# The copy of an attention block's weighed sums out of PSUM: from VectorE to ScalarE

## The chip, the cores and the metric

The kernel runs on one core of a Trainium2 chip. What is measured is the device time of one execution in microseconds (us), as the median of several runs. Five engines work side by side, each through its own instructions in order: TensorE (PE in the profile; its weight loads are listed apart as PEld), VectorE (DVE), ScalarE (ACT), GpSimd (POOL), and SyncE (SP), which here issues most DMAs. They wait for each other by semaphores.

## The reference

A transformer block on 2048 rows of width 576: LayerNorm, attention with 32 heads of 18 columns, and a gated feed-forward part.

```python
def _A_ref(x, wqkv, wo):
    B, S, D = x.shape                      # 1, 2048, 576
    H = 32; Dh = D // H                    # 18
    qkv = (x @ wqkv).reshape(B, S, 3, H, Dh).transpose(2, 0, 3, 1, 4)
    q, k, v = qkv[0], qkv[1], qkv[2]
    scores = jnp.einsum("bhqd,bhkd->bhqk", q, k) * Dh ** -0.5
    p = _softmax(scores, axis=-1)
    o = jnp.einsum("bhqk,bhkd->bhqd", p, v)
    return o.transpose(0, 2, 1, 3).reshape(B, S, D) @ wo

x = A_x
h = x + _A_ref(_layernorm(x), A_wqkv, A_wo)
h2 = h + _B_ref(_layernorm(h), B_w_gate, B_w_up, B_w_down)   # gelu(x@gate) * (x@up) @ down
```

## The kernel before

**Blocks and steps.** The attention is cut into 32 blocks: 8 groups of four heads, and in each group 4 chunks of 512 queries. The loop over `n` goes through the blocks, the loop over `kt` through 16 key steps of 128 keys. In a step TensorE makes four score tiles, one a head, keys down and queries across (L665, `score`), ScalarE turns each into its exponentials in the buffers `pes` (L667), and TensorE multiplies these with the values and adds the result to one PSUM bank, `acc`, which is `bank3` in the instructions (L673, `weigh`). The weighing of a step runs during the next step, in two halves of 256 queries. `acc` takes all 16 steps of a block; every head has 32 of its 128 rows, and the row behind a head's 18 sums holds the sum of its weights.

**Maxima.** Softmax needs a query's largest score. It comes from a second set of score tiles, queries down and keys across, which run one and a half blocks ahead (`maxima`, `max_bank`): TensorE makes the tile (L615), and VectorE reduces it to one maximum a row (L625). One tile in eight goes another way: ScalarE writes its Relu to SBUF (L619), and VectorE combines that with the partner tile in one instruction (L623). A block needs 64 such tiles, that is 48 reductions, 8 Relus and 8 combined instructions.

**PSUM.** The score tiles of both kinds share seven banks, taken in turn (`m_ring`: `bank0` to `bank2` and `quad0` to `quad3`). TensorE can write a tile into a bank only when ScalarE or VectorE is done with the tile of seven turns before.

**Order.** In this stage the order on PE, ACT, DVE and POOL is the order in which the program is written. Two strings set it, one for even and one for odd `kt`:

```python
STEPS = ("ssmsmmfwmsw", "mssmssmfwwm")
OUT_AT = STEPS[0].rindex("w")
```

Here `s` is a score tile with its exponential, `m` a tile for maxima with its reduction, `w` one half of the weighing, and `f` filling work. The last `w` of step 0 ends the weighing of the block before, and right behind it comes the first part of `out_block`, with the copy out of `acc` (L688). The next block's first weighing, which overwrites `acc`, is the first `w` of step 1; between them stand, in step 1, four scores and three tiles for maxima.

**What reads the copy.** `out_block` goes on in three parts. The copy's result `oT` is read by a DMA that picks out the sums of weights (L691); GpSimd inverts them (L698 and the lines behind it), two DMAs spread the result over the rows, and GpSimd multiplies and splits (L711 to L713), before SyncE sends the rows to `XT`. For the last two blocks the copy is already on ScalarE.

Of the kernel before, what the change touches and what calls it, by code (L numbers as in the profile page):

```python
# [31 lines left out]
def tile_block(  # L32
# [18 lines left out]
    nc = tc.nc  # L51
# [5 lines left out]
    TB = min(512, S)  # L57
# [624 lines left out]
    def out_block(n, acc):  # L682

        g, qc = divmod(n, NB)
        oT = oTs[n % 2]
        (nc.scalar.copy if n >= NS - 2 else nc.vector.tensor_copy)(oT, acc[:, :TB])  # L688
        R = 4 * TB // P
        rc = small.tile([P, R], F32, tag="rc", name="rc")  # L690
        (nc.scalar if n == NS - 1 else nc.sync).dma_start(rc, oT.rearrange("(h c) q -> h c q", c=32)[:, DH].rearrange(  # L691
            "h (p q) -> h p q", q=R))
        yield
        if n < NS - NB:
            den, rc = rc, small.tile([P, R], F32, tag="rp", name="rp")
            re = small.tile([P, R], F32, tag="re", name="re")
            for c in range(0, R, 4):
                nc.gpsimd.tensor_tensor(rc[:, c : c + 4], den[:, c : c + 4],  # L698
                                        minus_one.to_broadcast([P, 4]), op=ALU.pow)
            nc.gpsimd.tensor_mul(re, den, rc)  # L700
            nc.gpsimd.tensor_scalar(re, re, -1.0, 2.0, op0=ALU.mult, op1=ALU.add)
            nc.gpsimd.tensor_mul(rc, rc, re)
        else:
            nc.vector.reciprocal(rc, rc)
        rd = rc_dram[n % 2]
        nc.sync.dma_start(rd, rc)
        nc.sync.dma_start(rcb, rd.rearrange("(h p) q -> h (p q)", h=4).unsqueeze(1)
                         .to_broadcast([4, 32, TB]))
        yield
        if n < NS - 2:  # L710
            nc.gpsimd.tensor_mul(oT, oT, rcb)  # L711
            nc.gpsimd.tensor_copy(ohl[:, 0], oT)
            nc.gpsimd.tensor_sub(ohl[:, 1], oT, ohl[:, 0])  # L713
        else:
            nc.vector.tensor_mul(oT, oT, rcb)
            (nc.scalar.copy if n == NS - 1 else nc.vector.tensor_copy)(ohl[:, 0], oT)
            nc.vector.tensor_sub(ohl[:, 1], oT, ohl[:, 0])
        sl = slice(qc * TB, (qc + 1) * TB)
        for hh in range(4):
            f, end = (4 * g + hh) * DH, (4 * g + hh + 1) * DH  # L720
            r = 32 * hh
            while f < end:
                c, p = divmod(f, P)
                k = min(end - f, P - p)
                if c < NK:
                    nc.sync.dma_start(XT[p : p + k, c : c + NK + 2 : NK + 1, sl], ohl[r : r + k])
                else:
                    other = nc.gpsimd if n >= NS - 2 else nc.sync
                    nc.sync.dma_start(XT[p : p + k, NK, sl], ohl[r : r + k, 0])
                    other.dma_start(XT[TAIL + p : TAIL + p + k, NK, sl], ohl[r : r + k, 1])  # L730
                f += k
                r += k

    NS = NG * NB
# [525 lines left out]
    for n in range(NS):  # L1260
        g, qc = divmod(n, NB)
        acc = singles[3]
        late = n > NS - NB
        for kt in range(NT):
            heads = iter(range(4))
            halves = weigh(*prev) if prev is not None else iter(())
            for step_no, step in enumerate(STEPS[kt % 2]):
                if step == "s":
                    score(n, kt, next(heads))
                elif step == "m":  # L1270
                    take(mxs)
                elif step == "w":
                    take(halves)
                    if kt == 0 and step_no == OUT_AT and prev is not None:
                        ob = out_block(prev[0], prev[2])
                        next(ob)
                else:
                    if n < NS - 1 or kt < 11:
                        take(fill, 2)
                    take(side)  # L1280
# [29 lines left out]
    run(side)  # L1310
    run(weigh(*prev))
    ob = out_block(prev[0], prev[2])
    next(ob)
    for _ in fill:
# [103 lines left out]
```

## Time and profile before

| | |
|---|---|
| three runs | 2606.03, 2608.47, 2609.94 us; median 2608.47 us |
| profiled execution, first to last instruction | 2604.1 us |
| median of the runs less that span | 4.4 us |
| PE busy in the span | 2579.3 us (99%) |
| DVE busy | 2010.0 us (77%) |
| ACT busy | 1661.3 us (64%) |
| POOL busy | 818.9 us (31%) |
| copies at L688 on VectorE / on ScalarE | 30 / 2 |
| one such copy, from its start to its end | 681 ns on VectorE, 585 ns on ScalarE |

The profile's rows stand in a section below. Times there are in us from the span's start. Busy time counts an instruction from its start to its end; two instructions that follow each other on one engine can overlap, as the second may start before the first has ended, so the spacing of the ends of a row of instructions without a pause is the time that each one holds the engine. A row that ends in `x2` is two instructions, from the start of the first to the end of the second.

### The profile page before, as it was taken

Reading aid. Unit: us, or ns where it says so; the run is one execution under the profiler, and the core shown is the slowest. Engines: PE = TensorE matmul, PEld = TensorE weight load, DVE = VectorE, ACT = ScalarE, POOL = GpSimd, SP = SyncE. Lnnn points to the kernel's source line nnn. Section 1 sums busy time; section 2 is a strip of 40 time slices with the busy share of each in tenths; the row PEclk is TensorE's granted clock in tenths of the full one; section 3 lists DMA queues with packets and bytes.
Section 4 is the critical chain, followed back from the end, with each engine's and each line's share of the span. In section 5 each row is a group of like instructions: output and inputs, shape, how many; then the busy total and the mean of one; then the engine's idle time right before and its main releaser. Section 6 shows DMA issues by size and latency. Waiting matters only on the chain.

```text
span 2604.1 us, 53642 instructions
## 1 busy us (share of the span) xinstructions
PE 2579.3 (99%) x20765; PEld 1198.2 (46%) x20765; DVE 2010.0 (77%) x3886; ACT 1661.3 (64%) x3124; POOL 818.9 (31%) x1146
## 2 busy tenths in 40 slices
PE   8999999999999999999999999999999999999999
PEld 4543333333333333333335555555555555555555
DVE  8479999999999999999867675757565656565653
ACT  6229999999999999999774543424243433333332
POOL 4302532322223232324585432323232323222221
PEclk9999999999999999999999999999999999999999
DMA  8621010101001010101135410101010101010110
GB/s 227 154 77 45 17 47 17 44 19 39 20 23 41 16 43 16 47 16 32 38 64 116 83 34 30 34 30 34 30 34 30 34 30 34 30 34 30 34 56 37
DMA packets 170193, 118.23 MB, mean 45 GB/s; under 512 B 88664, under 2 KB 147564, under 8 KB 169938
## 3 DMA queue, kind: packets, MB, share of 16 engines
q1 hardware_dynamic: 161198, 98.47, 14.2%
q0 software_dynamic: 8608, 16.33, 2.6%
q8 instruction: 162, 2.65, 0.4%
q14 instruction: 93, 0.76, 0.1%
q10 hardware_dynamic: 132, 0.01, 0.0%
HBM read 80.05 MB, written 15.01 MB: 37 GB/s over the span
## 4 chain that ended last, share of the span: by engine, by line
PE 92%; DVE 4%; POOL 1%; DMA 1%; issue 1%; ACT 1%; SPq 0%; POOLq 0%; ACTq 0%
PE bank L673 19%; PE bank L1125 15%; PE more L1125 15%; PE bank L300 11%; PE more L300 8%; PE quad L615 7%; PE bank L615 6%; PE quad L300 4%; PE quad L665 4%; DVE mx L625 3%; PE bank L665 3%; DVE nat L688 1%; DMA A<-qk_hi 0%; POOL A L1055 0%; ACT A L155 0%
## 5 line engine op out<-in xcount | busy, mean ns | idle before, releaser
L667 ACT ACTIVATE WK<-quad 128x512 f32<-128x512 f32 x1170 | 656.2, 621 | 23.4 <-PE quad L665 21.0
L673 PE MATMUL bank<-WK,V 128*32 128x256 f32 x8192 | 606.6, 388 | 2.7 <-DVE nat L688 0.6
L625 DVE TENSOR_REDUCE mx<-quad 128x1 f32<-128x512 f32 x836 | 553.8, 684 | 9.0 <-PE quad L665 1.5
L667 ACT ACTIVATE WK<-bank 128x512 f32<-128x512 f32 x878 | 504.9, 622 | 11.1 <-PE bank L665 9.3
L625 DVE TENSOR_REDUCE mx<-bank 128x1 f32<-128x512 f32 x716 | 477.1, 684 | 33.5 <-PE bank L615 26.4
L300 PEld LDWEIGHTS <-WK 128*128 128x128 f16 x3456 | 338.2, 98 | 88.3
L1125 PEld LDWEIGHTS <-W 128*128 128x128 f16 x2394 | 234.3, 98 | 278.3
L673 PEld LDWEIGHTS bank<-WK,V 128*32 128x32 f32 x8192 | 190.0, 108 | 268.2 <-issue 201.3
L300 PE MATMUL more<-W,WK 128*128 128x288 f16 x1728 | 235.2, 286 | 0.0
L300 PE MATMUL bank<-W,WK 128*128 128x288 f16 x1728 | 235.2, 286 | 0.0
L698 POOL TENSOR_TENSOR rp<-rc,minus_one 128x4 f32<-128x4 f32 x112 | 111.2, 1012 | 383.9 <-DMA rc<-nat 383.9
L1125 PE MATMUL bank<-X,W 128*128 128x512 f16 x792 | 223.8, 379 | 0.0
L1125 PE MATMUL bank<-V,W 128*128 128x512 f16 x720 | 202.4, 379 | 0.0
L993 POOL TENSOR_TENSOR A<-A 128x384 f32<-128x384 f32 x136 | 138.1, 1036 | 200.2 <-DMA A<-in_B_w_up_dram 83.7
L615 PE MATMUL quad<-W 54*128 54x512 f16 x514 | 191.0, 382 | 0.2 <-DVE mx L625 0.2
L615 PEld LDWEIGHTS <-W 54*128 54x128 f16 x1024 | 74.5, 94 | 241.3 <-issue 226.8
L1139 POOL TENSOR_TENSOR WK<-tmp,WK 128x512 f16<-128x512 f32 x73 | 88.5, 1212 | 305.8 <-ACT WK L1136 305.6
L615 PEld LDWEIGHTS <-A 54*128 54x128 f16 x1024 | 71.1, 94 | 231.0 <-issue 216.7
L1143 ACT COPY tmp<-more 128x512 f32<-128x512 f32 x36 | 20.9, 582 | 238.3 <-PE more L1125 203.4
L665 PE MATMUL quad<-A 56*128 56x512 f16 x584 | 172.1, 380 | 0.3
L615 PE MATMUL quad<-A 54*128 54x512 f16 x462 | 171.6, 382 | 0.1
L665 PE MATMUL quad<-W 56*128 56x512 f16 x586 | 167.5, 380 | 0.1
(348 smaller groups left out, 4122.3 us busy)
## 6 DMA issues: line engine op xcount, KB each, us to landing
A<-in_B_w_down_dram SPq DMA_DIRECT2D x8, 1152.0 KB
nat<-rc SPq DMA_DIRECT2D x32, 256.0 KB
A<-in_B_w_gate_dram SPq DMA_DIRECT2D x64, 128.0 KB
A<-in_B_w_up_dram SPq DMA_DIRECT2D x64, 128.0 KB
qk_hi<-tmp SPq DMA_DIRECT2D x36, 128.0 KB
qk_lo<-tmp SPq DMA_DIRECT2D x36, 128.0 KB
out_dram<-nat SPq DMA_DIRECT2D x16, 288.0 KB
X<-nat SPq DMA_DIRECT2D x100, 36.0 KB
```

The source lines that it names most:

```text
L300: nc.tensor.matmul(dst, a, b, start=(i == 0), stop=(i == len(pairs) - 1))
L615: nc.tensor.matmul(pm[:, :TB], Q[r, q0 : q0 + P], keys, start=True, stop=True)
L625: nc.vector.tensor_reduce(dst, pm[:, :TB], axis=AX.X, op=ALU.max)
L665: nc.tensor.matmul(pS[:, :TB], K[r, kt * P : (kt + 1) * P], Q[r, qc * TB : (qc + 1) * TB], start=True, stop=True)
L667: nc.scalar.activation(pes[(2 * kt + hh // 2) % NPE][:, hh % 2], pS[:, :TB], AF.Exp, scale=ex_reg)
L673: nc.tensor.matmul(acc[32 * hh : 32 * hh + 32, qs], Vg[n // NB][:, kt * G4 + hh * VC : kt * G4 + hh * VC + 32], pes[(2 * kt + hh // 2) % N ...
L688: (nc.scalar.copy if n >= NS - 2 else nc.vector.tensor_copy)(oT, acc[:, :TB])
L698: nc.gpsimd.tensor_tensor(rc[:, c : c + 4], den[:, c : c + 4], minus_one.to_broadcast([P, 4]), op=ALU.pow)
L993: op(W8[:, d], W8[:, a], W8[:, b])
L1125: nc.tensor.matmul(bank, w, x_, start=start and i == 0, stop=i == len(mm) - 1, skip_group_check=not start)
L1139: nc.gpsimd.tensor_sub(hl[:, 2 * i + j], v, hh[:, 2 * i + j])
L1143: nc.scalar.copy(xg, g[0])
```

## The change

The condition at L688 is gone. Blocks 30 and 31 had their copy on ScalarE before and keep it there; for blocks 0 to 29 it moves from VectorE to ScalarE.

```diff
         g, qc = divmod(n, NB)
         oT = oTs[n % 2]
-        (nc.scalar.copy if n >= NS - 2 else nc.vector.tensor_copy)(oT, acc[:, :TB])
+        nc.scalar.copy(oT, acc[:, :TB])
         R = 4 * TB // P
```

On ScalarE, at the start of block 10, these rows stood in a row before: the fourth exponential of step 0 is the one that reads `quad3`, those behind it belong to steps 1 and 2 (`WK` holds `pes`, and `nat` the rows of the Relu).

```order
L667 ACTIVATE WK_81<-bank2_68 128x512
L619 ACTIVATE nat_77<-quad0_73 128x512
L667 ACTIVATE WK_81<-quad3_76 128x512
L667 ACTIVATE WK_81<-bank1_67 128x512
L667 ACTIVATE WK_81<-bank2_68 128x512
L667 ACTIVATE WK_81<-quad1_74 128x512
L667 ACTIVATE WK_81<-quad2_75 128x512
```

The same place now, where `nat` is also the buffer `oT`:

```order
L667 ACTIVATE WK_81<-bank2_68 128x512
L619 ACTIVATE nat_77<-quad0_73 128x512
L667 ACTIVATE WK_81<-quad3_76 128x512
L688 COPY nat_77<-bank3_69 128x512
L667 ACTIVATE WK_81<-bank1_67 128x512
L667 ACTIVATE WK_81<-bank2_68 128x512
L667 ACTIVATE WK_81<-quad1_74 128x512
L667 ACTIVATE WK_81<-quad2_75 128x512
```

The copy stands between the last exponential of step 0 and the four of step 1. On VectorE it leaves the place between two reductions, here at the start of the same block:

```order
 L625 TENSOR_REDUCE mx_6079<-quad1_74 128x1
 L625 TENSOR_REDUCE mx_6079<-quad2_75 128x1
-L688 COPY nat_77<-bank3_69 128x512
 L625 TENSOR_REDUCE mx_6079<-bank0_66 128x1
 L623 ISA nat_77,mx_6079<-quad0_73,nat_77 128x512
```

VectorE's other rows keep their order. TensorE's order is the same throughout; only the first weighing of a block, and the readers of `oT`, wait for ScalarE where they waited for VectorE.

## Rows read from the trace of the kernel before

**Rows 1.** The page: busy time by engine, and the chain that ended last by engine.
```profile
PE 2579.3 (99%) x20765; PEld 1198.2 (46%) x20765; DVE 2010.0 (77%) x3886; ACT 1661.3 (64%) x3124; POOL 818.9 (31%) x1146
PE 92%; DVE 4%; POOL 1%; DMA 1%; issue 1%; ACT 1%; SPq 0%; POOLq 0%; ACTq 0%
```

**Rows 2.** One attention block: PE, PEld, DVE, ACT, POOL busy; granted clock; DMA share; GB/s.
```profile
530.24:566.08 35.84, 35.76 (x388) 11.54 (x384) 35.32 (x67) 35.73 (x73) 8.37 (x14) 1.00 0.08 21
```

**Rows 3.** Line L688, who waited for it: us in total, times.
```profile
  PEld bank L673: 15.8, 31
```

**Rows 4.** ScalarE in order of time at a block's start: start, duration, what.
```profile
565.16 0.67 ACT L619 ACTIVATE nat<-quad 128x512 f32<-128x512 f32 x1
565.64 0.68 ACT L667 ACTIVATE WK<-quad 128x512 f32<-128x512 f32 x1
566.23 1.08 ACT L667 ACTIVATE WK<-bank 128x512 f32<-128x512 f32 x2
567.20 1.10 ACT L667 ACTIVATE WK<-quad 128x512 f32<-128x512 f32 x2
...
570.92 1.57 ACT L667 ACTIVATE WK<-quad 128x512 f32<-128x512 f32 x3
```

**Rows 5.** TensorE in order of time around the same block's start.
```profile
561.28 0.39 PE L665 MATMUL quad<-A 56*128 56x512 f16 x1
...
563.93 0.39 PE L615 MATMUL quad<-A 54*128 54x512 f16 x1
564.24 0.64 PE L673 MATMUL bank<-WK,V 128*32 128x256 f32 x8
...
565.71 0.60 PE L665 MATMUL bank<-A 56*128 56x512 f16 x2
...
566.38 0.38 PE L615 MATMUL quad<-A 54*128 54x512 f16 x1
...
566.82 1.07 PE L673 MATMUL bank<-WK,V 128*32 128x256 f32 x16
...
568.35 0.37 PE L615 MATMUL quad<-nat,A 54*128 54x512 f16 x1
568.63 0.37 PE L615 MATMUL quad<-A 54*128 54x512 f16 x1
568.93 0.64 PE L673 MATMUL bank<-WK,V 128*32 128x256 f32 x8
...
570.40 0.60 PE L665 MATMUL quad<-A 56*128 56x512 f16 x2
```

**Rows 6.** VectorE in order of time around the same block's start.
```profile
562.92 1.46 DVE L625 TENSOR_REDUCE mx<-quad 128x1 f32<-128x512 f32 x2
...
566.08 0.68 DVE L688 COPY nat<-bank 128x512 f32<-128x512 f32 x1
566.68 0.68 DVE L625 TENSOR_REDUCE mx<-bank 128x1 f32<-128x512 f32 x1
...
567.88 0.69 DVE L625 TENSOR_REDUCE mx<-quad 128x1 f32<-128x512 f32 x1
```

**Rows 7.** ScalarE in order of time around the copy of block 30.
```profile
1348.62 0.58 ACT L688 COPY nat<-bank 128x512 f32<-128x512 f32 x1
1349.10 1.09 ACT L667 ACTIVATE WK<-bank 128x512 f32<-128x512 f32 x2
```

**Rows 8.** ScalarE in order of time: a copy of the same size behind another instruction.
```profile
1397.31 1.26 ACT L1013 ACTIVATE W<-A,p_s_m 128x1152 f16<-128x1152 f32 x1
1398.46 0.58 ACT L1146 COPY tmp<-bank 128x512 f32<-128x512 f32 x1
```

**Rows 9.** TensorE at the starts of blocks 3 and 30, with idle time and its releaser.
```profile
315.34 0.39 PE L615 MATMUL quad<-W 54*128 54x512 f16 x1
315.93 0.84 PE L673 MATMUL bank<-WK,V 128*32 128x256 f32 x10 [0.21 <-DVE nat L688]
...
1301.96 0.64 PE L673 MATMUL bank<-WK,V 128*32 128x256 f32 x8 [0.21 <-DVE nat L688]
```

## The prediction, made before the changed kernel was run

> **What bounds the kernel now.** I read the page first, then the busy times of single attention blocks, then the three engines in order of time around a block's start. The page says that TensorE is busy 99% and carries 92% of the chain that ended last; VectorE has 4% of it and ScalarE 1% [rows 1]. That invites the thought that ScalarE has time to spare. It is an average over stages. In one attention block of 35.84 us TensorE, VectorE and ScalarE are busy 35.76, 35.32 and 35.73 us [rows 2]: all three look full, so busy time does not say which of them sets the pace. The granted clock is 1.00 there, and nothing in the change bears on it.
>
> Spacings tell more. ScalarE's four rows from 565.16 on end at 565.83, 566.32, 567.31 (two) and 568.30 (two) [rows 4]. The spacing of the ends is 0.49 us, and only between 566.32 and 567.31 is there a little more (0.99 for two, of which 0.01 to 0.02 is a pause). A double step has eight exponentials and one Relu, so ScalarE needs 9 x 0.49 = 4.41 us for it. TensorE's regular double step, from the first score of one odd step to that of the next, takes 565.71 - 561.28 = 4.43 us [rows 5]. **ScalarE is therefore full to about 0.02 us in a double step**, and tied to TensorE in a loop: the last tile for maxima of an even step is held until the fourth exponential of the odd step before has freed its bank (568.30 to 568.35, a hand-over of 0.05) [rows 4, 5], then come the weighing, the scores of the next odd step, and their exponentials. VectorE is behind in that race: it has pauses, for instance two reductions that take 1.46 us together [rows 6], where two without a pause would take 0.60 from start to start and 0.68 for the last, 1.28.
>
> At a block's start this pattern is broken. The double step from 565.71 to 570.40 takes 4.69 us, 0.26 more [rows 5]. Both parts of that are VectorE's: the first weighing waits for the copy, which ends at 566.76, and starts at 566.82, and because the copy delays the reductions by 0.60, the tile at 568.63 waits for the reduction that ends at 568.57, so that the second weighing starts at 568.93 [rows 5, 6]. In total 31 weight loads waited 15.8 us for L688 [rows 3]. That wait is what the change can win back.
>
> **The change part by part.** *Removed from VectorE:* 30 copies of 0.68 us, each holding it for 0.60 us (566.08 to 566.68) [rows 6]. VectorE's reductions at a block's start come 0.60 us earlier, and the tile at 568.63 no longer waits for one. Elsewhere VectorE waits for TensorE once or twice in a double step, so the time is not worth anything there.
>
> *Added to ScalarE:* 30 copies, each behind the fourth exponential of step 0. **How long one holds ScalarE** is shown by rows from other stages: behind an instruction that ends at 1398.57 the copy ends at 1399.04, 0.47 later [rows 8]; and the two exponentials behind a copy that ends at 1349.20 end at 1350.19, 0.495 each [rows 7]. I take 0.475, and 0.495 for the first exponential behind it. The sums are there in time: VectorE began to read them at 566.08 [rows 6], and ScalarE reaches the copy at about 566.12, 0.48 after the start at 565.64 [rows 4]. Queued behind the copy are the four exponentials of step 1, and behind those, through their banks, TensorE.
>
> *A regular block's start, laid out anew.* The fourth exponential of step 0 ends at 566.32 [rows 4]. The copy ends at 566.32 + 0.475 = 566.80, so the first weighing, 0.06 behind it as before, starts at 566.86 where it was 566.82. The four exponentials of step 1 end 0.495 + 3 x 0.49 = 1.965 later, at 568.76, where before it was 568.30: 0.46 late. The tile that waits for the fourth starts at 568.81. From the last tile to the weighing it is 564.24 - 563.93 = 0.31 us where nothing else is waited for [rows 5], which gives 569.12 in place of 568.93. **So a regular block gets longer by 0.19 us**: VectorE's two waits (0.26) are gone, and ScalarE's (0.45) stand in their place. Nothing later takes it back: the next double step's first score comes at 570.59, its exponential can start 0.52 later, as before (570.40 to 570.92) [rows 4, 5], and end 0.60 behind that, at 571.71; ScalarE's own queue would have it end at 568.76 + 6 x 0.49 = 571.70. Both engines are then 0.19 late, and the old rhythm goes on from there. Of the 30 moved copies 27 stand at such a start: 27 x 0.19 = +5.1 us.
>
> *Three irregular starts.* In blocks 3, 29 and 30 TensorE is already late for other reasons and ScalarE waits for it; there the copy fits into ScalarE's pause. The last tile stands at 315.34 and the weighing at 315.93 [rows 9], 0.59 apart, where 0.31 is the least: 0.28 is won. The second of VectorE's two waits may go too; at a regular start the first is 566.82 - 566.38 - 0.31 = 0.13 [rows 5], and the second the rest of 0.26, so 0.13 more. Of the three starts the first and the last stand in [rows 9]; all show the same idle 0.21 in front of the weighing. That is 0.28 to 0.41 each, -0.8 to -1.2; I take -1.0.
>
> *With one answer:* the readers of `oT` (the DMA at L691, GpSimd's L711) get it 0.04 us later and are not waited for within the block; the two copies that were on ScalarE before don't change; no DMA is moved.
>
> **Sum:** +5.1 - 1.0 = +4.1 us. On the profiled span that is 2604.1 + 4.1 = 2608.2; the median of the runs lies 4.4 above the span, so 2612.6 us, 0.16% more than 2608.47. A measurement of this kernel can tell about 0.2% (5.2 us) from no change.
>
> *Bounds.* The one price that no row shows in place is a copy within a full row of exponentials. From below: if starts and not ends were what counts, the copy and each exponential would take 0.48; step 1's first exponential would start at 566.60 in place of 566.23, the delay would be 0.37, the weighing at 569.03, and the sum 27 x 0.10 - 1.0 = +1.7. From above: if the copy held ScalarE for its whole 0.58 us [rows 7], a block would lose 0.30, and the sum would be 27 x 0.30 - 0.8 = +7.3. The row nearest to the place is that of [rows 8], a copy behind a busy ScalarE; it gives the value taken. The ends drift away from the starts, by some 0.01 an instruction, until the next pause: 0.67 and 0.68 long at 565.16 and 565.64 [rows 4], against 0.60 behind a pause. So the engine is slower than its starts say, and I stay with the ends. The Trainium skill (Perfetto Trace Analysis, Per-instruction lifecycle) has the profiled end behind the write's acknowledgement, and lets the next instruction begin to fetch before that, once the one before has executed; by that reading the starts would be the better clock, and the sum +1.7.
>
> **The rivals.** *A, slower: the copy holds ScalarE for its whole run.* Place: the four exponentials behind it. Price: +7.3 us, 2615.8. It decides when the hold passes 0.515 us, since 27 x (hold - 0.285) - 1.0 reaches 5.2 there. For it: no row shows a copy in a full row of exponentials, and the forecast lies only 1.1 us below the point. Against it: the row in which the next exponential starts 0.48 behind the copy's start [rows 7].
>
> *B, faster: VectorE sets the pace.* Then 0.60 us comes free in each of 30 blocks: -18 us, 2590. For it: it is the only other engine with a share in the chain [rows 1], and 35.32 of 35.84 us busy [rows 2]. Against it: the pauses in [rows 6]. The Trainium skill (Perfetto Trace Analysis, Optimizing Scalar/DVE Operations) advises moving work to ScalarE where VectorE is saturated; by that this change would be rival B, but [rows 4] show ScalarE at least as full.
>
> *C, faster: the waits of the block's start vanish and ScalarE catches up.* 27 x 0.26 + 1.0 = 8.0 us less, 2600.5. It needs ScalarE to make up 0.46 us within one double step, where the rows leave it 0.02; it holds only if exponentials can come closer together than 0.49, which I have not seen in a full stretch.
>
> **How the numbers follow.** The forecast's case has 0.55, A (with all that lies above 0.2%) 0.33, C 0.08, B 0.04. The time is that of the forecast, 2612.6. Its own range is that of the bounds' nearer part, 2610 to 2613.7 (0.2%). The range of 8 in 10 reaches up to A and a little beyond, 2617, and down to where the runs scatter below the lower bound (+1.7 is 2610), 2606.5; B and C, 0.12, are left out. Faster by over 0.2%: B and C, 0.12. Slower by over 0.2%: A, 0.33. Within: 0.55.
>
> **What the profile of the changed kernel would show.** At a regular start no weight load waits for VectorE's L688, and ScalarE's row reads exponential, copy, exponentials with ends 0.47 to 0.48 and 0.49 apart. The double step with the copy takes 4.88 us in place of 4.69, all others 4.43, and a block 36.03 in place of 35.84. VectorE shows pauses at the block's start. I am wrong if the double step takes 4.43 to 4.6 (C), if blocks get shorter by more than 0.3 (B), or if the copy's end lies over 0.515 behind the end before it (A).

## The result, and the profile after

The changed kernel takes 2613.36 us (median of 15 runs, 2611.23 to 2617.86), the kernel before 2608.47 (median of 15, 2606.03 to 2612.63). The ratio is 1.002, with an interval from 1.0013 to 1.0028, so the change costs between 3.4 and 7.3 us. Forecast were +4.1 us and 2612.6. The kernel is slower beyond the scatter; whether by more or less than 0.2% the interval does not say.

The page of the changed kernel, span, busy time and chain by engine:

```profile
span 2615.4 us, 53644 instructions
PE 2585.5 (99%) x20765; PEld 1200.8 (46%) x20765; DVE 2002.3 (77%) x3856; ACT 1670.4 (64%) x3154; POOL 818.5 (31%) x1146
PE 93%; ACT 2%; DMA 1%; DVE 1%; POOL 1%; issue 1%; SPq 1%; ACTq 0%; POOLq 0%; DVEq 0%
```

Beside [rows 1] VectorE has lost its share of the chain (4% to 1%) and ScalarE has gained one. The span has grown by 11.3 us, more than the median (4.9). The first score tiles of the blocks, in both traces, say where:

| stretch | before | after | difference |
|---|---|---|---|
| to the first score of block 0 | 202.90 | 205.09 | +2.2 |
| block 0 | 37.13 | 40.06 | +2.9 |
| blocks 1 to 28 | 1004.50 | 1010.09 | +5.6 |
| block 29 to the last step of block 31 | 132.45 | 133.67 | +1.2 |
| the rest, to the last instruction | 1227.12 | 1226.46 | -0.7 |

The first copy that was moved runs in block 1, so what lies ahead of it is not the change. Among the experiments below that alter only this copy (e3 to e6, and e12), block 0 begins from 201.8 to 203.2 and takes 37.1 to 38.7 us; the last section says what lengthened it here. **The change itself is in the third line.** That line holds 27 times 0.21 us, less 0.46 won in block 3, and some 0.4 of scatter: blocks 14, 21 and 28 of the changed kernel took 0.1 to 0.3 longer than their neighbours, and block 15 before it 0.3.

A stretch of one block, as in [rows 2], in the same columns (PE, PEld, DVE, ACT, POOL busy; clock; DMA share; GB/s), and who waits for the copy (us, times):

```profile
533.55:569.60 36.05, 35.82 (x388) 11.72 (x385) 35.04 (x66) 36.02 (x75) 8.38 (x14) 1.00 0.09 22
```
```profile
L688 ACT COPY nat<-bank x32: 586/677/678, 248.0 to 1392.6; 128x512 f32<-128x512 f32 x32
...
  PEld bank L673: 15.3, 29
```

A block takes 36.05 us in place of 35.84. TensorE's loads still wait for the copy as long as in [rows 3] (15.3 us in 29 waits, 15.8 in 31 before): the wait has changed its engine, not its size. It is not a price either, as e3 shows below.

ScalarE at the start of block 10, to be held against [rows 4]:

```profile
571.99 0.68 ACT L667 ACTIVATE WK<-quad 128x512 f32<-128x512 f32 x1
572.46 0.68 ACT L688 COPY nat<-bank 128x512 f32<-128x512 f32 x1
572.93 1.20 ACT L667 ACTIVATE WK<-bank 128x512 f32<-128x512 f32 x2
573.90 1.21 ACT L667 ACTIVATE WK<-quad 128x512 f32<-128x512 f32 x2
574.85 1.24 ACT L667 ACTIVATE WK<-bank 128x512 f32<-128x512 f32 x2
```

TensorE there, against [rows 5]:

```profile
572.05 0.60 PE L665 MATMUL bank<-A 56*128 56x512 f16 x2
...
572.72 0.38 PE L615 MATMUL quad<-A 54*128 54x512 f16 x1
573.19 1.07 PE L673 MATMUL bank<-WK,V 128*32 128x256 f32 x16
...
575.17 0.39 PE L615 MATMUL quad<-A 54*128 54x512 f16 x1
575.48 0.64 PE L673 MATMUL bank<-WK,V 128*32 128x256 f32 x8
...
576.95 0.60 PE L665 MATMUL quad<-A 56*128 56x512 f16 x2
```

And VectorE, against [rows 6], with the idle time in front of an instruction and its releaser in brackets:

```profile
573.69 0.68 DVE L625 TENSOR_REDUCE mx<-quad 128x1 f32<-128x512 f32 x1
574.62 0.69 DVE L625 TENSOR_REDUCE mx<-bank 128x1 f32<-128x512 f32 x1 [0.25 <-PE bank L665]
```

The last exponential of step 0 ends at 572.67, the copy at 573.14, the four exponentials behind it at 574.13 (two) and 575.11 (two). The weighing starts 0.05 behind the copy, at 573.19. The last tile for maxima starts 0.06 behind the fourth exponential, at 575.17, and the second weighing 0.31 later. VectorE, no longer late, waits for TensorE. The double step takes 576.95 - 572.05 = 4.90 us; it was 4.69.

### The profile page after: what moved, and what is told of

Same layout as the page of the kernel before. It is cut to its first block, busy times and chain, and to the rows that moved or that the text cites. A ratio compares the mean times of both kernels' runs of the same rounds, so it can differ in the third digit from the quotient of the medians.

```text
span 2615.4 us, 53644 instructions
## 1 busy us (share of the span) xinstructions
PE 2585.5 (99%) x20765; PEld 1200.8 (46%) x20765; DVE 2002.3 (77%) x3856; ACT 1670.4 (64%) x3154; POOL 818.5 (31%) x1146
## 4 chain that ended last, share of the span: by engine, by line
PE 93%; ACT 2%; DMA 1%; DVE 1%; POOL 1%; issue 1%; SPq 1%; ACTq 0%; POOLq 0%; DVEq 0%
PE bank L673 19%; PE bank L1125 15%; PE more L1125 15%; PE bank L300 11%; PE more L300 8%; PE quad L615 8%; PE bank L615 6%; PE quad L300 5%; PE quad L665 4%; PE bank L665 3%; ACT WK L667 2%; DVE mx L625 0%; DMA A<-qk_hi 0%; SPq L729 0%; DMA nat<-qk_hi 0%
## 5 line engine op out<-in xcount | busy, mean ns | idle before, releaser
L667 ACT ACTIVATE WK<-quad 128x512 f32<-128x512 f32 x1170 | 665.7, 636 | 23.1 <-PE quad L665 21.7
L667 ACT ACTIVATE WK<-bank 128x512 f32<-128x512 f32 x878 | 513.5, 636 | 12.3 <-PE bank L665 11.6
```

Of the source, the lines that this page charges most:

```text
L667: nc.scalar.activation(pes[(2 * kt + hh // 2) % NPE][:, hh % 2], pS[:, :TB], AF.Exp, scale=ex_reg)
```

## The experiments

The theory is that a block's length is set by a path that goes from ScalarE's exponentials over the freed PSUM banks to TensorE's tiles and weighings and back, and that the copy on ScalarE lies on it with its whole hold. The rivals: the loss is a hand-over at the block's start, not ScalarE's time (H); it is the sum of ScalarE's work in a block, wherever it stands (S); VectorE sets the pace (V).

"Block" below is the time from the first score of block 10 to that of block 11, "start" the double step of steps 1 and 2. Before and after stand for comparison; medians are in us, with the median of the kernel before from the same chip, and e8 to e11 are single runs, of which the blocks are read and not the times.

| kernel | block 10 from, to | block | start | median, before beside it |
|---|---|---|---|---|
| before | 563.26, 599.10 | 35.84 | 4.69 | |
| after | 569.60, 605.65 | 36.05 | 4.90 | 2613.36, 2608.47 |
| e1 | 569.42, 605.87 | 36.45 | 4.69 | 2626.14, 2608.89 |
| e2 | 571.22, 607.63 | 36.41 | 4.69 | 2623.22, 2608.89 |
| e3 | 561.36, 596.99 | 35.63 | 4.48 | 2602.55, 2608.89 |
| e4 | 564.98, 601.09 | 36.11 | 4.96 | 2616.32, 2609.08 |
| e5 | 567.11, 603.25 | 36.14 | 4.99 | 2616.32, 2609.08 |
| e6 | 564.40, 600.24 | 35.84 | 4.69 | 2608.15, 2609.08 |
| e7 | 568.77, 604.81 | 36.04 | 4.90 | 2613.99, 2608.89 |
| e8 | 563.58, 599.30 | 35.72 | 4.57 | 2605.87, 2609.39 |
| e9 | 569.25, 605.58 | 36.33 | 4.68 | 2622.33, 2609.39 |
| e10 | 570.06, 606.33 | 36.27 | 4.69 | 2621.13, 2609.39 |
| e11 | 565.71, 601.79 | 36.08 | 4.68 | 2613.22, 2609.39 |
| e12 | 561.16, 596.74 | 35.58 | 4.43 | 2601.26, 2608.67 |

### What each copy costs: eight columns on ScalarE (e3) and on VectorE (e12)

e3, against the kernel after; in e12 the same edit is made to VectorE's copy of the kernel before:

```diff
-nc.scalar.copy(oT, acc[:, :TB])
+C = TB if n >= NS - 2 else 8
+nc.scalar.copy(oT[:, :C], acc[:, :C])
```

> The changed kernel, with 8 of 512 columns copied in blocks 0 to 29 (the rest of the sums is not copied, so the rows behind it are computed from old values); the copy's place, its waits and who waits for it stay. Theory, full row: the copy's cost goes with the time it holds ScalarE; the double step at the block's start falls from 4.90 to 4.43 to 4.50 us, a block to 35.60 to 35.67, 5 to 7 us less than before the change. Rival, hand-over: the waits stay, so the double step stays near 4.9 and the time near that of the changed kernel, +5 us.

> The kernel before, with 8 of 512 columns copied by VectorE in blocks 0 to 28 and 29 (the rest of the sums is not copied, so the rows behind it are computed from old values). It prices VectorE's copy as the run with 8 columns on ScalarE priced ScalarE's. If VectorE's copy costs the 0.26 us that I had put down to its two waits, a block takes 35.58 to 35.65 us, and the whole 6 to 8 us less than before. If ScalarE and TensorE alone set the length of a block and VectorE's copy only stood beside them, 35.84.

e3 gave a ratio of 0.9978 (0.9968 to 0.9987), e12 0.9976 (0.9966 to 0.9986). ScalarE in e3, at the start of block 10, and VectorE in e12:

```profile
563.74 0.68 ACT L667 ACTIVATE WK<-quad 128x512 f32<-128x512 f32 x1
564.22 0.26 ACT L689 COPY nat<-bank 128x8 f32<-128x8 f32 x1
564.33 1.14 ACT L667 ACTIVATE WK<-bank 128x512 f32<-128x512 f32 x2
```
```profile
563.98 0.16 DVE L689 COPY nat<-bank 128x8 f32<-128x8 f32 x1
564.06 0.68 DVE L625 TENSOR_REDUCE mx<-bank 128x1 f32<-128x512 f32 x1
```

In e3 the place, the waits and the waiting instructions are those of the changed kernel; only the hold is short (564.42 to 564.48), and the block falls from 36.05 to 35.63. H is out: it is the time on ScalarE that costs. e12's start takes 4.43 us, the regular double step, so 35.58 is a block without any price for the copy. Against it **VectorE's copy costs 0.26 us a block and ScalarE's 0.47**, which is its hold. In e3 TensorE's loads still wait 10.2 us for the copy, in 27 waits, while a block costs only 0.05 us more than in e12: the sum of these waits does not measure what the copy costs.

### One instruction more on ScalarE in mid-block (e1, e9)

In e1, made from the kernel before, the Relu of step 12 runs twice, with the same input and output; in e9 the added line is the same with `row2` for its output and `tmp3[:, 0]` for its input.

```diff
 nc.scalar.activation(row, pm[:, :TB], AF.Relu)
+if (t, kc) == (1, 1):
+    nc.scalar.activation(row, pm[:, :TB], AF.Relu)
```

> The kernel before, with the copy left on VectorE, and one Relu a block, the one of step 12 in the middle of the block, run twice over the same buffer. Theory, full row: ScalarE has no time to spare anywhere in a block, so one more instruction of 0.49 us costs about 0.45 us a block wherever it stands: block 36.3 us in place of 35.84, +13 us in all. Rival, hand-over: what the changed kernel lost comes from ScalarE and TensorE waiting for each other at a block's start; an instruction in mid-block then costs 0 to 0.05 us a block, under 2 us. Rival, VectorE paces: 0.

> The kernel before, with one more Relu of 512 columns a block on ScalarE in step 12, from a buffer in SBUF that nothing writes in this stage, into a buffer of its own, so that it waits for nothing and holds no PSUM bank. In the run with the Relu repeated over its own output the second one waited for the first and held ScalarE 0.63 us; the block got 0.61 longer. Full row: the cost is again the hold less about 0.02, that is 0.45 to 0.52 us a block if the hold is 0.47 to 0.54. If the cost of that run was the waiting and not the hold, 0 to 0.1 us.

e1's ratio is 1.0066 (1.005 to 1.0083), more than expected: a block is 0.61 longer, not 0.45. ScalarE in e1, and in e9, where the line of the added instruction is L621 in both:

```profile
598.31 0.67 ACT L619 ACTIVATE nat<-bank 128x512 f32<-128x512 f32 x1
599.01 0.60 ACT L621 ACTIVATE nat<-bank 128x512 f32<-128x512 f32 x1
```
```profile
598.13 0.67 ACT L619 ACTIVATE nat<-bank 128x512 f32<-128x512 f32 x1
598.61 0.70 ACT L621 ACTIVATE row<-tmp 128x512 f16<-128x512 f32 x1
```

In e1 the second Relu writes what the first has written, waits in the built program for a semaphore that ScalarE itself raises, and starts only after the first one's end (598.98, 599.01); its end is 0.63 behind the first one's. Held 0.63, lost 0.61. In e9 it waits for nothing and its end is 0.51 behind the first one's (598.80, 599.31); lost are 0.49. Both lose the hold less 0.02, the slack that the prediction had read between ScalarE's 4.41 us and the double step of 4.43. So an instruction added in step 12 costs as much of its hold as the copy does at the block's start: ScalarE is full at both places.

### Less work on ScalarE, behind and ahead of the copy (e7, e8)

e7, against the kernel after; in e8 the steps are (2, 1) for the short Relu and (2, 0) for the maxima without it:

```diff
-nc.scalar.activation(row, pm[:, :TB], AF.Relu)
+some = 8 if n and (t, kc) == (2, 3) else TB
+nc.scalar.activation(row[:, :some], pm[:, :some], AF.Relu)
 ...
-nc.vector.tensor_tensor_reduce(row, pm[:, :TB], row, 1.0, LOWEST, ALU.add, ALU.max, dst)
+if (t, kc) == (2, 2):
+    nc.vector.tensor_reduce(dst, pm[:, :TB], axis=AX.X, op=ALU.max)
+else:
+    nc.vector.tensor_tensor_reduce(row, pm[:, :TB], row, 1.0, LOWEST, ALU.add, ALU.max, dst)
```

> The changed kernel, with one Relu a block, that of step 2 just behind the copy's four exponentials, cut to 8 columns (its tile is left out of the maxima; the partner tile is reduced alone). ScalarE then has in each block about as much work as before the change. If only the sum of ScalarE's work in a block counts, the block goes back to 35.6 to 35.85 us, some 6 us under the changed kernel. If what counts is the path from the copy over the four exponentials of step 1 to TensorE, the Relu behind them is not on it: the block stays at 36.0 to 36.05, and ScalarE shows the 0.4 us as a pause in front of step 3.

> The changed kernel, with the Relu of step 0, just ahead of the copy, cut to 8 columns (its tile is left out of the maxima; the partner tile is reduced alone). Path theory: ScalarE can reach the copy up to 0.45 us earlier, but the last weighing ends only about 0.2 us before the copy's start of now, so the copy and the exponentials behind it gain 0.2 us and a block falls from 36.05 to about 35.85 us. If the sum of ScalarE's work in a block were what counts, 35.6; if the copy's place in the row does not matter, 36.05.

e7's ratio is 1.0022 (1.0012 to 1.0031), the changed kernel's over again, and its blocks are as long. ScalarE in e7, from the short Relu on, and in e8, from the last exponential ahead of the copy (its copy is L692):

```profile
575.44 0.37 ACT L620 ACTIVATE nat<-quad 128x8 f32<-128x8 f32 x1
575.68 0.63 ACT L671 ACTIVATE WK<-bank 128x512 f32<-128x512 f32 x1
576.63 1.57 ACT L671 ACTIVATE WK<-quad 128x512 f32<-128x512 f32 x3 [0.33 <-PE quad L669]
```
```profile
565.59 0.63 ACT L671 ACTIVATE WK<-quad 128x512 f32<-128x512 f32 x1
566.20 0.58 ACT L692 COPY nat<-bank 128x512 f32<-128x512 f32 x1
566.68 1.09 ACT L671 ACTIVATE WK<-bank 128x512 f32<-128x512 f32 x2
567.65 1.11 ACT L671 ACTIVATE WK<-quad 128x512 f32<-128x512 f32 x2
```

With the Relu behind the copy cut short, ScalarE idles 0.33 us in front of step 3, waiting for TensorE's score, and nothing is won. With the one ahead of it cut short, the block falls by 0.33 to 35.72. S is out: nearly the same work is left out in both, and only the one on the path pays. In e8 the copy starts 0.17 behind the first score of step 1 (566.03), where in the changed kernel it is 0.41 (572.46 - 572.05). That is 0.24, a little more than the 0.2 expected; the other 0.09 is that the copy and the exponentials behind a short pause no longer carry the drift of a full row (the copy takes 0.58 in place of 0.68).

### One instruction more on VectorE (e2, e10, e11)

In the kernel before, e2 repeats a reduction, with the same input and output; e10 adds at the same place one of another tile, shown here, and e11 has it with `h` 2:

```diff
 nc.vector.tensor_reduce(dst, pm[:, :TB], axis=AX.X, op=ALU.max)
+if n and (t, kc, h) == (1, 0, 1):
+    nc.vector.tensor_reduce(mx2, tmp3[:, 0], axis=AX.X, op=ALU.max)
```

> The kernel before, with one reduction a block, in step 12, run twice into the same place: 0.60 us more on VectorE. Theory, full row on ScalarE: VectorE has small pauses in each double step, and the cost is what its delay cost at the block's start, about 0.13 us a block, +4 us in all (0 to 0.3 us a block). Rival, VectorE paces: the whole 0.60 us a block, +17 us.

> The kernel before, with one more reduction of 512 columns a block on VectorE, from an SBUF buffer into a place of its own, behind the first reduction of step 12, where it stands ahead of the reductions for which TensorE waits in the next step. If VectorE's slack there is 0.15 us, as the run with the repeated reduction says (0.72 us more, 0.57 lost), the block gets 0.45 us longer. By the pauses that I had read in the trace it would be 0.13.

> The same reduction behind the fourth reduction of step 12, followed by a plain reduction and the combined instruction as the copy of the kernel before is at a block's start. Place theory: the copy cost VectorE's partners little because it stood behind the reduction that TensorE waits for first; here the cost is 0.1 to 0.25 us a block, against about 0.45 at the first place. If the place makes no difference, both give the same.

e2's ratio is 1.0054 (1.0038 to 1.0071), and here the expectation failed: 0.57 us a block, not 0.13. VectorE in e2, and in e10 and e11:

```profile
598.63 1.29 DVE L625 TENSOR_REDUCE mx<-quad 128x1 f32<-128x512 f32 x2
599.95 0.69 DVE L627 TENSOR_REDUCE mx<-quad 128x1 f32<-128x512 f32 x1
600.56 0.68 DVE L625 TENSOR_REDUCE mx<-bank 128x1 f32<-128x512 f32 x1
```
```profile
598.67 0.68 DVE L627 TENSOR_REDUCE mx<-tmp 128x1 f32<-128x512 f32 x1
599.26 0.68 DVE L625 TENSOR_REDUCE mx<-bank 128x1 f32<-128x512 f32 x1
```
```profile
595.51 0.67 DVE L627 TENSOR_REDUCE mx<-tmp 128x1 f32<-128x512 f32 x1
596.10 0.68 DVE L625 TENSOR_REDUCE mx<-quad 128x1 f32<-128x512 f32 x1
```

The repeated reduction in e2 waited for its twin (599.92, 599.95), whose place it writes again: its end is 0.72 behind the other's. 0.72 more, 0.57 lost, so VectorE had 0.15 us to give. e10, without that wait, adds 0.59 and loses 0.43: 0.16. So VectorE is nearly as full as ScalarE. e11 adds the same 0.59 three reductions further on, where the copy of the kernel before stood at a block's start, and loses 0.24. So the place decides, and 0.60 us of copying at the block's start, between the same reductions, cost a similar 0.26. My reading is that behind the reduction for which TensorE waits next, a delay has the time up to the following wait to shrink; no run takes that apart. V is not what the change shows: VectorE's freed time is worth 0.26 us at that place and no more (e12).

### Splitting the copy between the engines (e4, e5)

e4, with halves in blocks 0 to 29, against the kernel after; in e5 ScalarE takes 128 columns and VectorE the rest:

```diff
-nc.scalar.copy(oT, acc[:, :TB])
+nc.scalar.copy(oT[:, :256], acc[:, :256])
+nc.vector.tensor_copy(oT[:, 256:], acc[:, 256:TB])
```

> The copy of blocks 0 to 29 split by columns: 256 on ScalarE, 256 on VectorE. Path theory, with the hold of each half worked out from the whole one (ScalarE 0.05 + 256 x 0.00083 = 0.26 us, VectorE 0.07 + 256 x 0.00104 = 0.33): ScalarE's four exponentials are 0.24 late in place of 0.46, which puts the second weighing 0.03 before where it is with the copy on VectorE; a block of 35.80 to 35.85 us, and 1 to 3 us less than before the change. If two engines that must both have finished cost the waits of both, a block is as long as the changed one or longer, 36.05 to 36.3.

> The same split with 128 columns on ScalarE and 384 on VectorE, where the delay that each engine brings to the second weighing is the same by the estimate (ScalarE 0.16 us held, VectorE 0.47): the second weighing comes 0.13 us earlier than before the change, a block of about 35.70, and 3 to 5 us less than before the change. If the waits of both add up, a block of 35.9 or more.

Both were slower than the kernel before, with ratios of 1.003 (1.002 to 1.004) and 1.0029 (1.0018 to 1.0041). Their blocks, 36.11 and 36.14 us, are longer than with either whole copy (35.84 and 36.05); the times alone cannot tell them from the changed kernel's ratio of 1.002. ScalarE, VectorE and TensorE in e4:

```profile
567.83 0.46 ACT L691 COPY nat<-bank 128x256 f32<-128x256 f32 x1
```
```profile
568.33 0.42 DVE L692 COPY nat<-bank 128x256 f32<-128x256 f32 x1 [0.45 <-ACT nat L691]
568.67 0.68 DVE L625 TENSOR_REDUCE mx<-bank 128x1 f32<-128x512 f32 x1
```
```profile
568.81 1.07 PE L673 MATMUL bank<-WK,V 128*32 128x256 f32 x16 [0.34 <-DVE nat L692]
```

The holds were as estimated (ScalarE's half ends 0.26 behind the exponential that ends at 568.03, VectorE's goes from 568.33 to 568.67). But the halves don't run side by side: in the built program VectorE's half waits for ScalarE's. VectorE stands idle for 0.45 us, and the weighing waits for the two in a row. Both halves read one PSUM bank and write one buffer; which of the two made the program put them in a row, and whether it had to, no run shows.

### ScalarE's copy at the three irregular starts alone (e6)

```diff
-(nc.scalar.copy if n >= NS - 2 else nc.vector.tensor_copy)(oT, acc[:, :TB])
+(nc.scalar.copy if n in (2, 28, 29) or n >= NS - 2 else nc.vector.tensor_copy)(oT, acc[:, :TB])
```

> The kernel before, with the copy on ScalarE in the three irregular starts alone (the copies of blocks 2, 28 and 29, made at the starts of blocks 3, 29 and 30) and on VectorE elsewhere. Block 3 gets about 0.45 us shorter, as in the changed kernel; block 29's 0.42 is given back where TensorE waits for the rows that GpSimd prepares; block 30's 0.5 is given back in part. In all 0.5 to 1 us less, which the times cannot tell from no change.

The ratio is 0.9997 (0.9988 to 1.0006), as expected no difference that can be told. Block 3 goes from 36.51 to 36.05 us, as in the changed kernel. In blocks 29 and 30 TensorE's wait for rows in step 12 grows, from 1.77 to 2.19 us and from 0.71 to 1.04: the first takes back all of the 0.42 won, the second 0.33 of the 0.50.

## Why the prediction held, and where it didn't

**What bounds the kernel: right.** Busy time and the chain's shares gave no answer; the spacing of the ends did. The slack of 0.02 us in a double step was found again in e1 and e9, to the hundredth. One step was read wrongly, without a part in the sum: the 15.8 us of waiting loads are not what the change could win back. Without a price for the copy (e12) a block is 0.26 us shorter, some 7 us in 27 blocks.

**A regular start: right, term by term.** The rebuilt start can be laid over the trace if 6.34 us is taken off, the difference between the first scores of step 1 (572.05 and 565.71). Copy's end: predicted 566.80, measured 566.80. First weighing: 566.86, 566.85. Fourth exponential's end: 568.76, 568.77. Last tile: 568.81, 568.83. Second weighing: 569.12, 569.14. Next double step: 570.59, 570.61. A block gets 0.21 us longer where 0.19 was forecast: 27 x 0.21 = 5.7 us in place of 5.1. The hold of 0.475 us, the one price without a row in its place, was measured at 0.47. That also settles rival A, which needed 0.515 or more, and C, which needed ScalarE to catch up. The sum by starts, +1.7 us, which went with the reading of the Trainium skill (Perfetto Trace Analysis, Per-instruction lifecycle), would have made the double step 4.79; it was 4.90. For the starts that sum was right: on the same scale the first exponential behind the copy starts at 566.59, where it gave 566.60. But the ends are 0.47 late and the starts 0.36, and TensorE's tile follows the end of the fourth exponential, by 0.06.

**The three irregular starts: the mechanism right, the size off on both sides.** Counting the first four steps, the starts gain 0.46 (block 3), 0.42 (block 29) and 0.50 us (block 30), more than the 0.28 to 0.41 forecast. But in block 29 the gain is given back. There TensorE must wait for rows that GpSimd and the DMAs of that block prepare; the first matmul behind the wait, in the kernel before and in the changed one:

```profile
1276.85 0.41 PE L300 MATMUL quad<-W,X 128*128 128x288 f16 x2 [1.77 <-POOL A L1044]
```
```profile
1287.57 0.47 PE L300 MATMUL quad<-W,X 128*128 128x288 f16 x2 [2.20 <-DMA X<-nat]
```

Block 29 begins at 1244.53 and at 1255.24, so the rows come 32.32 and 32.33 us into the block either way, and what the start won is waited away 0.43 us longer. Block 30 loses part of its gain in the same way (the wait of its step 12 grows from 0.71 to 1.07): behind that step it stands at 32.76 and 32.62 us, 0.14 won in place of 0.50. So of the term's -1.0 some -0.6 is left. With 5.7 that makes +5.1 us, beside 4.9 measured. What failed in this term is that a gain at a start was counted as kept to the block's end. How much of block 30's is kept is not settled: in e7, with the same copies, that wait is 1.72 us, and nothing is left of the gain.

**VectorE's pauses: wrong, without harm to the sum.** I had read them as room, and called VectorE behind in the race. It has 0.15 to 0.16 us in a double step, not the 0.47 that my expectation for e2 took; the cost of VectorE's copy at the block's start is low because of where it stood (e11), not because VectorE had time. For the change itself it made no difference, since it takes work off VectorE. Rival B falls all the same: with the copy all but gone from every engine (e12) a block is 0.26 us shorter, not 0.60.

**The advice to move work** from a saturated VectorE to ScalarE, which the prediction took from the Trainium skill (Perfetto Trace Analysis, Optimizing Scalar/DVE Operations), does not fit here: the same copy costs 0.26 us a block on VectorE and 0.47 on ScalarE (e12 against before and after), although ScalarE has the shorter hold.

None of the kernels that compute the whole of the reference as the kernel before does it was measurably faster than that kernel. e8 points to where a gain could lie, a block of 35.72 us with one Relu less in front of the copy, but it leaves a part of the maxima out.

## What to carry to other kernels

Where several engines are busy throughout, take the hold of an instruction from the spacing of the ends in a row without pauses, and compare the engines' sums over one period; a few hundredths of a microsecond of slack can decide whether an instruction more is free or costs all of its hold. Then look at the place: on VectorE the same added reduction cost 0.43 of its 0.59 us at one place and 0.24 at another (e10, e11), and on ScalarE a Relu taken away where nobody waited gave nothing back (e7). A gain ahead of a wait for something with its own clock, such as a chain of DMAs, is lost there.

## What the runs showed of the hardware that was not expected

An instruction that overwrites what the one before it on the same engine has just written did not overlap with it: ScalarE's hold was 0.63 us in place of 0.49, VectorE's 0.72 in place of 0.60 (e1, e2). In both, it waits in the built program for a semaphore of its own engine; the added instructions of e9 and e10, with another output, wait for none. So the order is the program's; whether the chip would need it was not tried.

TensorE's clock fell to its lower level, 1.2 GHz, in stretches of the profiled run of the changed kernel. Its times by stretch, in the columns of [rows 2], around the start of block 0 and in block 29:

```profile
206.00:208.00 2.00, 0.83 (x4) 0.20 (x4) 2.00 (x4) 1.99 (x3) 0.00 (x0) 1.00 0.60 150
208.00:210.00 2.00, 1.67 (x7) 0.44 (x6) 1.16 (x3) 2.00 (x6) 0.00 (x0) 0.79 0.41 125
210.00:212.00 2.00, 2.00 (x18) 0.59 (x16) 1.23 (x3) 1.62 (x4) 0.00 (x0) 0.50 0.32 86
...
1287.50:1291.00 3.50, 3.43 (x24) 0.83 (x26) 1.21 (x2) 0.60 (x1) 1.93 (x2) 0.54 0.05 12
```

Ahead of the fall in block 0 TensorE was busy for 0.83 of 2 us, waiting for VectorE and ScalarE; ahead of that in block 29 it had waited 2.20 us for rows. The granted clock then stood at 0.50 from 210 to 212 us, and at 0.54 on average over the stretch in block 29, while TensorE worked. In e7 the same wait in block 29 lasted 2.19 us, and the clock stayed at 1.00. So the same pause does not always bring the fall, and this is a part of the scatter between executions: block 29's step 12 took 7.98 us here and 6.81 in e7. The whole of block 0, in the kernel before and in the changed one:

```profile
202.90:240.03 37.13, 35.32 (x370) 11.50 (x369) 34.87 (x66) 36.97 (x74) 6.71 (x16) 1.00 0.18 47
```
```profile
205.09:245.15 40.06, 38.25 (x369) 11.77 (x369) 35.19 (x66) 37.21 (x74) 6.72 (x16) 0.91 0.17 44
```

The mean granted clock was 1.00 before and 0.91 here, and block 0 took 2.9 us longer. The experiments that alter only the copy agree: with a mean clock of 1.00 from 196 to 246 us block 0 took 37.07 us (e4), with 0.97 it took 38.64 (e3, e6). So block 0's difference goes with the clock; the change's first copy comes only behind it.
